# FNet and gMLP on one core: the first two DFT blocks loaded in halves, two tiles for each of the first rows of x

## The chip, the cores and the metric

The kernel runs on one core of one Trainium2 chip. The metric is the device time of one execution in microseconds (us). Five engines work side by side, each through its own instructions in the order written: the tensor engine (PE in the profile, its weight loads PEld), the vector engine (DVE), the scalar engine (ACT), GpSimd (POOL) and the sync engine (SP), which here only issues transfers. The transfers between memory and the core's own memory run beside them (DMA).

## The reference

Two layers with adaptive layer norms, of which the first concerns us: an FNet layer that takes the real part of a two-dimensional Fourier transform, written as products with DFT matrices. S is 2048, D is 512, all in float32.

```python
h = _layernorm(x, axis=-1) * (1 + ca) + sa
# _A_ref(h, ...):
a = jnp.einsum("bsd,ed->bse", x, dft_hid_re)
b = jnp.einsum("bsd,ed->bse", x, dft_hid_im)
y = jnp.einsum("ts,bse->bte", dft_seq_re, a) - jnp.einsum("ts,bse->bte", dft_seq_im, b)
...
x = x + ga * _A_ref(h, A_dft_seq_re, A_dft_seq_im, A_dft_hid_re, A_dft_hid_im)
h = _layernorm(x, axis=-1) * (1 + cb) + sb
x = x + gb * _B_ref(h, B_w_in, B_w_sp, B_b_sp, B_w_out)
```

`_B_ref` is a gMLP block (a projection with GELU, a gate through a 2048 x 2048 matrix, a projection back). It comes later in the kernel and the change does not touch it.

## The kernel before

The kernel multiplies along the sequence first: g = C x, for the real matrix `cr` and the imaginary one `ci`, where x is only normalized (scale and shift are folded into later matrices). A matrix is cut into blocks of 512 x 512; block b of the list `src` is the real part when b is even and the imaginary part when b is odd, as long as the first 512 output rows (t = 0) are made. Each block gives four **tiles**: tile n is a slice of 128 sequence positions, n = 4 b + k. Tile n is multiplied with row block s of x ("row s", 128 sequence positions by 512), and adds to four accumulators, one for each 128 columns of x. For t = 0 tiles 0 to 3 are the real tiles of rows 0 to 3, tiles 4 to 7 the imaginary tiles of the same rows, tiles 8 to 11 the real tiles of rows 4 to 7, and so on.

Float32 is reached in three passes of a faster format: both operands are split into a high and a low half, and high x high, high x low and low x high are added. So one tile takes 12 matmuls with 128 x 512, three for each accumulator. For tiles 0 to 3 (`n < 4` in `mm_a`, line 520 of the profile) they are ordered in three groups of four: first all four with `ah` and `hh`, then with `al` and `hh`, then with `ah` and `hl`. From tile 4 on `matmul3` (lines 96 to 98) gives three passes for one accumulator after the other.

What a tile needs:

- `prep_hi(n)`: the tile is transposed from the loaded block (`stage`) into `t` (DVE, L189), and ACT makes its high half `ah` (L268). With the fourth tile of a block the block's buffer is given up and the load of block b + 2 is issued (`load`). Two blocks fit, two `t`, four `ah`, three `al`.
- `prep_lo(n)`: DVE makes the low half `al` (L286).

What a row needs: statistics on DVE (`stats_first` L438 to L441 for rows 0 to 3, `stats_x` L104 to L106 for later ones), two or three small POOL instructions, its high half `hh` on ACT (`hi_first`, L459, with one column set by `one_first`, L465), the normalized row `xn` on ACT (`norm_x`, L120) and its low half `hl` on DVE (`lo_h`, L501).

The order of all this is written by hand (a manual schedule): up to the first tile a straight list of calls, which the diff shows, then a loop over tiles. In the loop, `prep(n)` calls `prep_hi(n + 3)` and `prep_lo(n + 2)`, `mm_a(n)` issues the matmuls, and `run(n)` issues whatever was put there by `at(n, f, ...)`. Loads of rows are issued by `load_x(g, ks)`, of blocks by `load`, or by `load_half`, which takes 64 of the 128 columns that the staged block has per partition and row group: pieces of 256 B where `load` has 512 B. The first two tiles of a block lie in its first half.

Of the kernel before, what the change touches and what calls it, by code (L numbers as in the profile page):

```python
# [8 lines left out]
F32 = mybir.dt.float32  # L9
# [4 lines left out]
P = 128  # L14
# [5 lines left out]
def fnet_gmlp_kernel(  # L20
# [32 lines left out]
    nc = tc.nc  # L53
# [5 lines left out]
    NS = S // P  # L59
# [14 lines left out]
    blocks = ctx.enter_context(pool("blocks"))  # L74
# [49 lines left out]
    def at(n, f, *a):  # L124
        fill.setdefault(n, []).append((f, a))
# [6 lines left out]
    def quad(a, r, k):  # L132
        return a[r * Q:(r + 1) * Q, k * Q:(k + 1) * Q]

    src = []
    for t in range(NQ):
        for g, j in ([(g, j) for g in range(NQ) for j in range(2)] if t == 0 else
                     [(g, j) for j in range(2) for g in range(NQ)]):
            src.append(quad((cr, ci)[j], t, g))
    N2 = 4 * len(src)  # L140
    N1 = N2 + 8
    YPROD = (6, 7, 4, 5, 3)
    N3 = N1 + 4 * len(YPROD)
    N4 = N3 + 4 * len(YPROD)
# [3 lines left out]
    NB0 = len(src) + 2  # L148
    stage, T, AH, AL = {}, {}, {}, {}
# [6 lines left out]
    def load_half(tile_, a, h, engs=(nc.sync,) * 4):  # L156

        v = a.rearrange("(b j) (a s) -> a j b s", j=32, a=4)
        for q in range(4):
            engs[q].dma_start(tile_[32 * q:32 * q + 32], v[q][:, :, 64 * h:64 * h + 64])  # L160
# [3 lines left out]
    def load(b):  # L164
        if b < len(src):
            stage[b] = blocks.tile([P, 16, P], F32, tag="stage", bufs=2, name=f"stage{b}")
            load_block(stage[b], src[b])
        elif b < len(src) + 2:
            j = b - len(src)
            XB.append(blocks.tile([P, 4, Q], F32, tag="stage", bufs=2, name=f"xb{j}"))  # L170
            for g in range(2):
                nc.sync.dma_start(XB[j][:, 2 * g:2 * g + 2], ht_d[g].rearrange("(k p) t -> p k t", p=P)[:, 2 * j:2 * j + 2])
                for kk in range(2):
                    TT[2 * j + kk, g] = XB[j][:, 2 * g + kk]
        elif 4 * (b - NB0) < NE - N4:
            i, gh = divmod(b - NB0, NQ)
            g, h = divmod(gh, 2)
            p = PROD[i]
            stage[b] = blocks.tile([P, 2, 16, 64], F32, tag="stage", bufs=2, name=f"stage{b}")
            for r in range(2):  # L180
                load_half(stage[b][:, r], s_d[S_OF[p], r, g] if p in S_OF else
                          quad(w_sp, r + (2 if p == 4 else 0), g + (2 if p == 1 else 0)), h)
# [68 lines left out]
    def prep_hi(n):  # L251
        if n >= NE or n in highs:
            return
        highs.add(n)
        if N2 <= n < N4:
            T[n] = form_t(n)
        else:
            b, k = divmod(n, 4) if n < N2 else (NB0 + (n - N4) // 4, (n - N4) % 4)
            if b != NB0:
                T[n] = blocks.tile([P, Q], F32, tag="t", bufs=2, name=f"t{n}")  # L260
            if b == NB0:
                assert n in T
            elif n >= N4:
                squares(T[n], stage[b][:, k % 2], k // 2)
            else:
                squares(T[n], stage[b], k)
        AH[n] = SE[2][:, n - N4] if N4 <= n < N4 + 4 else blocks.tile([P, Q], F32R, tag="ah", bufs=4, name=f"ah{n}")
        nc.scalar.activation(AH[n], T[n], AF.Copy)  # L268
        if not N2 <= n < N4 and k == 3:
            stage.pop(b)  # L270
            if b != NB0:
                load(b + 2)


    def prep_lo(n):
        if n >= NE or n in lows:
            return
        lows.add(n)
        if N2 <= n < N4 and n % 4 == 3:
            AL[n] = slot(0, f"al{n}", F32R) if slots else zrow[0].tile([P, Q], F32R, tag="z1u", bufs=6, name=f"al{n}")  # L280
        elif N4 <= n < N4 + 4:
            AL[n] = slot(9 + n - N4, f"al{n}", F32R)
        else:
            AL[n] = blocks.tile([P, Q], F32R, tag="al", bufs=3, name=f"al{n}")
        t = T.pop(n)
        nc.vector.tensor_tensor(AL[n], t, AH[n].bitcast(F32), op=ALU.subtract)  # L286
# [132 lines left out]
    X, XG, LN, NRM, h_hi, h_lo = {}, {}, {}, {}, {}, {}  # L419

    def load_x(g, ks=range(4), eng=nc.sync):

        if g not in XG:
            XG[g] = spool.tile([P, 4, D], F32, tag="x", bufs=2, name=f"x{g}")
        k0, k1 = ks[0], ks[-1] + 1
        v = x.rearrange("(g a k i) d -> g a i k d", g=NQ, a=4, i=32)
        for a in range(4):
            eng.dma_start(XG[g][32 * a:32 * a + 32, k0:k1, :], v[g, a][:, k0:k1, :])
        for k in ks:
            X[4 * g + k] = XG[g][:, k, :]  # L430
# [4 lines left out]
    def stats_first(s):  # L435

        m = spool.tile([P, 12], F32, tag="first", bufs=4, name=f"first{s}")
        nc.vector.bn_stats(m[:, :6], X[s])  # L438
        mv = m[:, 8:]
        nc.vector.bn_aggr(mv[:, :2], m[:, :6])  # L440
        nc.vector.tensor_scalar(mv[:, 1:2], mv[:, 1:2], EPS, None, op0=ALU.add)  # L441
        nc.gpsimd.tensor_tensor(mv[:, 2:3], mv[:, 1:2], mhalf, op=ALU.pow)
        nc.gpsimd.tensor_scalar(mv[:, 3:4], mv[:, 0:1], mv[:, 2:3], -1.0, op0=ALU.mult, op1=ALU.mult)
        NRM[s] = mv[:, 2:3], mv[:, 3:4]
# [11 lines left out]
    def hi_first(s):  # L456
        h_hi[s] = hpool.tile([P, ND, P], F32R, name=f"hh{s}")
        h = h_hi[s].rearrange("p k (a i) -> p k a i", i=32)
        nc.scalar.activation(h, X[s].rearrange("p (a k i) -> p k a i", a=4, i=32), AF.Identity,  # L459
                             bias=NRM[s][1], scale=NRM[s][0])  # L460
        if s:
            one_first(s)
# [19 lines left out]
    def norm_x(s):  # L482

        if s not in LN:
            LN[s] = spool.tile([P, D], F32, tag="xn", bufs=4, name=f"xn{s}")
        if s > 1:
            nc.gpsimd.memset(LN[s][:, 0:1], 1.0)
        apply(LN[s][:, 1:], X.pop(s)[:, 1:], NRM.pop(s))

# [8 lines left out]
    def lo_h(s):  # L498
        h_lo[s] = hpool.tile([P, ND, P], F32R, name=f"hl{s}")
        lo, h = parts_h(s, h_lo)  # L500
        nc.vector.tensor_tensor(lo, h, parts_h(s, h_hi)[0].bitcast(F32), op=ALU.subtract)  # L501
        LN.pop(s)


    GP, gt_hi, gt_lo, YP = {}, {}, {}, {}
# [2 lines left out]

    def mm_a(n):
        t, r = divmod(n, 8 * NQ)  # L510
        j, s = ((r // 4) % 2, r // 8 * 4 + r % 4) if t == 0 else (r // NS, r % NS)
        if s == 0:
            for k in range(ND):
                GP[t, j, k] = bank(4 * j + k if t == 0 else ring[0] % 6, f"gp{t}_{j}_{k}")
                ring[0] += t > 0
        ah, al = AH.pop(n), AL.pop(n)
        if n < 4:
            for a, b in ((h_hi[s], ah), (h_hi[s], al), (h_lo[s], ah)):
                for k in (1, 2, 3, 0):
                    nc.tensor.matmul(GP[0, 0, k], a[:, k, :], b, start=s == 0 and b is ah and a is h_hi[s], stop=False)  # L520
            return
        for k in range(ND):
            matmul3(GP[t, j, k], h_hi[s][:, k, :], h_lo[s][:, k, :], ah, al, s == 0, s == NS - 1)
        if s == NS - 1:
            for k in range(ND):
                ps = GP.pop((t, j, k))
                gt_hi[t, j, k] = GP_[0].tile([P, Q], F32R, tag=f"gh{j}_{k}", name=f"gh{t}_{j}_{k}")
                gt_lo[t, j, k] = GP_[0].tile([P, Q], F32R, tag=f"gl{j}_{k}", name=f"gl{t}_{j}_{k}")
                split(gt_hi[t, j, k], gt_lo[t, j, k], ps)
# [524 lines left out]
    load_half(stage[0][:, :, :64], src[0], 0, two)  # L1054
    load_two(1)
    nc.scalar.activation(sc, ones[:, :ND], AF.Silu)
    load_x(0, range(2, 4))
    load_half(stage[0][:, :, 64:], src[0], 1)
    load(1)
    load_x(1, range(2))  # L1060
    keep_busy(4, 5)
    for s in range(2):
        LN[s] = spool.tile([P, D], F32, tag="xn", bufs=4, name=f"xn{s}")
        nc.gpsimd.memset(LN[s][:, 0:1], 1.0)
    stats_first(0)
# [3 lines left out]
    stats_first(1)  # L1069
    prep_lo(0)  # L1070
    norm_x(0)
    prep_hi(1)
    lo_h(0)
    hi_first(1)
    stats_first(2)
    prep_lo(1)
    norm_x(1)
    prep_hi(2)
    lo_h(1)
    hi_first(2)  # L1080
    stats_first(3)
    prep_lo(2)
    norm_x(2)
    prep_hi(3)
    hi_first(3)
    norm_x(3)
    at(0, lo_h, 2)
    at(1, lo_h, 3)
    at(0, load_x, 1, range(2, 4))
    at(2, load_row)  # L1090
    at(9, silu_row)
# [31 lines left out]
    for j, turn, weigh, row, fold, hi in ((0, (25, 26, 27, 28), (29, 29, 30, 30), 26, (34, 34, 35, 36), (40, 37, 38, 39)),  # L1123
# [8 lines left out]
        n = weigh[3] + 1  # L1132
# [20 lines left out]
    for t in range(NQ):  # L1153
        n = 8 * NQ * (t + 1)
# [136 lines left out]
    for i, p in enumerate(PROD):  # L1291
        for k in range(8):
            n = NB[p] + 2 * k
# [11 lines left out]
    for f in range(NF):  # L1305
        n = N4 + 24 + 8 * f
# [109 lines left out]
```

## Time and profile before

| | |
|---|---|
| median of three runs | 933.13 us (932.32 to 933.69) |
| the profiled execution | 932.66 us |
| its span in the profile | 930.9 us |
| PE busy | 924.6 us, 99% |
| DVE busy | 737.3 us, 79% |
| first matmul of tile 0 / of tile 4 | 7.30 us / 20.59 us after the span's start |

Times in the profile count from the start of the span. A row of the timeline has the start, the duration, the engine, the line of the kernel, the operation with its output and inputs, and in brackets how long the engine was idle before it and what ended that. The difference of 1.76 us between span and time lies outside the profiled span.

### The profile page before, as it was taken

What the parts mean: (1) busy time and instruction counts of PE and PEld (TensorE: products, weight loads), DVE (VectorE), ACT (ScalarE), POOL (GpSimd) and SP (SyncE); (2) the same over time, 40 slices, a digit from 0 to 9 for tenths busy, and PEclk for the clock granted to TensorE, in tenths of its full rate; (3) what the DMA queues carried; (4) which work ended last, traced back from release to release, by engine and by line L of the source; (5) the groups of instructions that cost most, each with busy time, mean ns of one, the idle gap of its engine ahead of it and who ended that gap; (6) DMA issues with size and microseconds to landing.
All of it is one profiled execution on the core that took longest, in us unless ns stands there. A gap on an engine that the chain in (4) does not pass through costs nothing.

```text
span 930.9 us, 12343 instructions
## 1 busy us (share of the span) xinstructions
PE 924.6 (99%) x4053; PEld 760.7 (82%) x4053; DVE 737.3 (79%) x1217; ACT 409.6 (44%) x734; POOL 198.9 (21%) x376
## 2 busy tenths in 40 slices
PE   8999999999999999999999999999999999999998
PEld 5888888888888888888888888888888888888886
DVE  7789967788687677875668788899799789896762
ACT  5685424232132221322577877674544544331121
POOL 2420000224654165323512320331000000000000
PEclk9999999999999999999999999999999999999999
DMA  9995762856639977996464764444464555744651
GB/s 215 219 226 123 146 158 46 192 148 163 165 86 306 306 207 222 277 337 232 138 217 135 273 204 103 118 106 104 104 147 102 132 140 138 177 102 149 188 174 57
DMA packets 246976, 157.88 MB, mean 170 GB/s; under 512 B 140384, under 2 KB 214368, under 8 KB 246784
## 3 DMA queue, kind: packets, MB, share of 16 engines
q1 hardware_dynamic: 233248, 119.57, 52.0%
q0 software_dynamic: 12272, 36.86, 11.5%
q10 hardware_dynamic: 1392, 0.66, 0.2%
q8 instruction: 32, 0.52, 0.2%
q14 instruction: 32, 0.26, 0.1%
HBM read 120.33 MB, written 36.71 MB: 169 GB/s over the span
## 4 chain that ended last, share of the span: by engine, by line
PE 98%; DMA 1%; DVE 0%; SPq 0%; issue 0%; ACTq 0%; POOL 0%; ACT 0%; DVEq 0%
PE gp L96 12%; PE gp L97 12%; PE gp L98 12%; PE gw L97 10%; PE gw L98 10%; PE gw L96 10%; PE yp L98 3%; PE yp L96 3%; PE yp L97 3%; PE op L98 3%; PE op L97 3%; PE op L96 3%; PE fp L97 1%; PE fp L98 1%; PE fp L96 1%; PE z2s L98 1%
## 5 line engine op out<-in xcount | busy, mean ns | idle before, releaser
L268 ACT ACTIVATE ah<-t 128x512 fp32r<-128x512 f32 x236 | 149.1, 632 | 364.7 <-DVE t L189 252.5
L286 DVE TENSOR_TENSOR al<-t,ah 128x512 fp32r<-128x512 f32 x236 | 160.7, 681 | 52.6 <-PE gp L97 27.9
L97 PE MATMUL gp<-al,hh 128*128 128x512 f32 x496 | 193.0, 389 | 0.0
L96 PE MATMUL gp<-ah,hh 128*128 128x512 f32 x496 | 193.0, 389 | 0.0
L98 PE MATMUL gp<-ah,hl 128*128 128x512 f32 x496 | 192.9, 389 | 0.0
L189 DVE STREAM_TRANSPOSE t<-stage 128x512 f32<-128x512 f32 x236 | 165.7, 702 | 11.2 <-DMA stage<-in_A_dft_seq_re_dram 4.9
L97 PE MATMUL gw<-al,bh 128*128 128x512 f32 x400 | 155.6, 389 | 0.0
L98 PE MATMUL gw<-ah,bl 128*128 128x512 f32 x384 | 149.5, 389 | 0.0
L96 PE MATMUL gw<-ah,bh 128*128 128x512 f32 x384 | 149.4, 389 | 0.0
L98 PEld LDWEIGHTS gp<-ah,hl 128*128 128x128 f32 x496 | 93.1, 188 | 19.4
L96 PEld LDWEIGHTS gp<-ah,hh 128*128 128x128 f32 x496 | 93.1, 188 | 19.4
L97 PEld LDWEIGHTS gp<-al,hh 128*128 128x128 f32 x496 | 93.1, 188 | 19.4 <-DVE al L286 0.2
L97 PEld LDWEIGHTS gw<-al,bh 128*128 128x128 f32 x400 | 75.1, 188 | 15.5
L98 PEld LDWEIGHTS gw<-ah,bl 128*128 128x128 f32 x384 | 72.1, 188 | 15.5 <-DVE bl L919 0.5
L96 PEld LDWEIGHTS gw<-ah,bh 128*128 128x128 f32 x384 | 72.1, 188 | 15.0
L891 POOL DMA_DIRECT2D s_d<-sj x64 | 35.1, 548 | 106.8 <-DVE sj L883 82.4
L96 PE MATMUL yp<-hth,gh 128*128 128x512 f32 x128 | 49.8, 389 | 0.0
L97 PE MATMUL yp<-htl,gh 128*128 128x512 f32 x128 | 49.8, 389 | 0.0
L98 PE MATMUL yp<-hth,gl 128*128 128x512 f32 x128 | 49.8, 389 | 0.0
L636 POOL DMA_DIRECT2D ht_d<-hturn x62 | 41.0, 667 | 23.9 <-DVE hturn L632 18.5
L96 PE MATMUL op<-woh,uh 128*128 128x512 f32 x112 | 43.6, 389 | 0.0
L97 PE MATMUL op<-wol,uh 128*128 128x512 f32 x112 | 43.6, 389 | 0.0
(233 smaller groups left out, 1446.0 us busy)
## 6 DMA issues: line engine op xcount, KB each, us to landing
stage<-in_A_dft_seq_im_dram SPq DMA_DIRECT2D x64, 256.0 KB, 5.6
sj<-in_B_w_sp_dram SPq DMA_DIRECT2D x32, 512.0 KB, 6.8
s_d<-sj POOLq DMA_DIRECT2D x64, 256.0 KB, 4.2
stage<-s_d SPq DMA_DIRECT2D x128, 128.0 KB, 2.8
stage<-in_A_dft_seq_re_dram SPq DMA_DIRECT2D x60, 256.0 KB, 5.4
stage<-in_B_w_sp_dram SPq DMA_DIRECT2D x88, 128.0 KB, 2.9
wm<-in_w_mod_dram SPq DMA_DIRECT2D x16, 256.0 KB, 6.1
xr<-in_A_x_dram POOLq DMA_DIRECT2D x16, 256.0 KB, 4.5
```

Of the source, the lines that this page charges most:

```text
L96: nc.tensor.matmul(acc, ah, bh, start=first, stop=False, skip_group_check=go_on)
L97: nc.tensor.matmul(acc, ah, bl, start=False, stop=False, skip_group_check=go_on)
L98: nc.tensor.matmul(acc, al, bh, start=False, stop=last, skip_group_check=go_on)
L189: nc.vector.transpose(dst.rearrange("p (b i) -> p b i", i=32), block[:, :, 32 * k:32 * k + 32])
L268: nc.scalar.activation(AH[n], T[n], AF.Copy)
L286: nc.vector.tensor_tensor(AL[n], t, AH[n].bitcast(F32), op=ALU.subtract)
L636: eng.dma_start(v[a, i], ht[32 * a:32 * a + 32].rearrange("c (b r) -> c b r", r=32))
L891: nc.gpsimd.dma_start(s_d[m, r, g][b * P:(b + 1) * P, :], a)
```

## The change

The first two blocks are loaded half by half, in the order: first half of block 0, first half of block 1, rows 2 and 3 of x, second half of block 0, second half of block 1. The list `PAIRED` gives the first eight tiles a new meaning (block, slice): tiles 0 and 1 are the real and imaginary tile of row 0, tiles 2 and 3 those of row 1, tiles 4 and 5 the real tiles of rows 2 and 3, tiles 6 and 7 their imaginary ones. The grouped order of matmuls holds for tiles 0 to 5. The calls ahead of the loop, and those of the first three turns, are ordered anew; the first four `xn` are allocated, and their first columns set, ahead of everything. The fourth tile of block 0 is now tile 5, so the load of block 2 is issued there.

```diff
+    PAIRED = ((0, 0), (1, 0), (0, 1), (1, 1), (0, 2), (0, 3), (1, 2), (1, 3))
...
-            b, k = divmod(n, 4) if n < N2 else (NB0 + (n - N4) // 4, (n - N4) % 4)
+            b, k = PAIRED[n] if n < 8 else divmod(n, 4) if n < N2 else (NB0 + (n - N4) // 4, (n - N4) % 4)
...
-        if s > 1:
+        if s > 3:
             nc.gpsimd.memset(LN[s][:, 0:1], 1.0)
...
-        j, s = ((r // 4) % 2, r // 8 * 4 + r % 4) if t == 0 else (r // NS, r % NS)
+        j, s = PAIRED[n] if n < 8 else ((r // 4) % 2, r // 8 * 4 + r % 4) if t == 0 else (r // NS, r % NS)
...
-        if n < 4:
+        if n < 6:
             for a, b in ((h_hi[s], ah), (h_hi[s], al), (h_lo[s], ah)):
                 for k in (1, 2, 3, 0):
-                    nc.tensor.matmul(GP[0, 0, k], a[:, k, :], b, start=s == 0 and b is ah and a is h_hi[s], stop=False)
+                    nc.tensor.matmul(GP[0, j, k], a[:, k, :], b, start=s == 0 and b is ah and a is h_hi[s], stop=False)
             return
...
     load_half(stage[0][:, :, :64], src[0], 0, two)
     load_two(1)
     nc.scalar.activation(sc, ones[:, :ND], AF.Silu)
+    stage[1] = blocks.tile([P, 16, P], F32, tag="stage", bufs=2, name="stage1")
+    load_half(stage[1][:, :, :64], src[1], 0)
     load_x(0, range(2, 4))
     load_half(stage[0][:, :, 64:], src[0], 1)
-    load(1)
+    load_half(stage[1][:, :, 64:], src[1], 1)
     load_x(1, range(2))
     keep_busy(4, 5)
-    for s in range(2):
+    for s in range(4):
         LN[s] = spool.tile([P, D], F32, tag="xn", bufs=4, name=f"xn{s}")
         nc.gpsimd.memset(LN[s][:, 0:1], 1.0)
     stats_first(0)
...
     stats_first(1)
     prep_lo(0)
     norm_x(0)
+    lo_h(0)
     prep_hi(1)
-    lo_h(0)
     hi_first(1)
+    prep_lo(1)
+    prep_hi(2)
     stats_first(2)
-    prep_lo(1)
     norm_x(1)
-    prep_hi(2)
+    prep_lo(2)
     lo_h(1)
+    prep_hi(3)
     hi_first(2)
-    stats_first(3)
-    prep_lo(2)
-    norm_x(2)
-    prep_hi(3)
-    hi_first(3)
-    norm_x(3)
-    at(0, lo_h, 2)
-    at(1, lo_h, 3)
+    at(0, prep_lo, 3)
+    at(0, norm_x, 2)
+    at(0, prep_hi, 4)
+    at(0, stats_first, 3)
+    at(1, prep_lo, 4)
+    at(1, lo_h, 2)
+    at(1, hi_first, 3)
+    at(1, norm_x, 3)
+    at(2, lo_h, 3)
     at(0, load_x, 1, range(2, 4))
```

## The prediction

> **What bounds the kernel now.** I read the page's head first, then the waits of the tensor engine, then its timeline over the first 22 us, and then the timelines of the engines that feed it there.
>
> ```profile
> span 930.9 us, 12343 instructions
> PE 924.6 (99%) x4053; PEld 760.7 (82%) x4053; DVE 737.3 (79%) x1217; ACT 409.6 (44%) x734; POOL 198.9 (21%) x376
> ...
> PE gp L520 <- DVE hl L501: 0.7, 1, 0.7
> ...
> PEld gp L520 <- DVE hl L501: 2.1, 3, 1.1
> ...
> 7.30 1.19 PE L520 MATMUL gp<-ah,hh 128*128 128x512 f32 x4
> 8.74 1.20 PE L520 MATMUL gp<-al,hh 128*128 128x512 f32 x4 [0.26 <-DVE al L286]
> 9.94 1.20 PE L520 MATMUL gp<-ah,hl 128*128 128x512 f32 x4
> 10.98 1.12 PE L520 MATMUL gp<-ah,hh 128*128 128x512 f32 x4
> ...
> 17.84 1.08 PE L520 MATMUL gp<-ah,hh 128*128 128x512 f32 x4
> 18.76 1.08 PE L520 MATMUL gp<-al,hh 128*128 128x512 f32 x4
> ...
> 20.59 0.39 PE L96 MATMUL gp<-ah,hh 128*128 128x512 f32 x1
> ...
> 21.27 0.39 PE L96 MATMUL gp<-ah,hh 128*128 128x512 f32 x1
> ...
> 927.17 0.60 ACT last L1039
> ```
>
> The tensor engine is the bound. From 20.59 to 21.27 it starts three matmuls: 0.227 us each. From 20.59, where the fifth tile begins, to 927.17, where ACT takes up the last result, 906.6 us pass; of the 4053 matmuls 8 keep the engine busy at the start and 48 belong to the first four tiles, so 3997 remain, 0.2268 us each. Nothing stands behind 20.59 that could be won. Ahead of it, the first 48 matmuls need 48 x 0.227 = 10.9 us and take 20.59 - 7.30 = 13.3 us. So **2.4 us** is all that this change can win as long as the first matmul stays at 7.30: 0.26% of the profiled execution's 932.66 us. The stalls are waits for the vector engine (DVE): the weight loads waited three times, 2.1 us in all, for hl, the low half of a row of x.
>
> The change feeds each of rows 0 and 1 of x to two tiles, so that a row's preparation is needed half as often. Whether that helps is decided by DVE, whose instructions run in the order written:
>
> ```profile
> 8.01 0.68 DVE L286 TENSOR_TENSOR al<-t,ah 128x512 fp32r<-128x512 f32 x1
> 8.61 0.70 DVE L189 STREAM_TRANSPOSE t<-stage 128x512 f32<-128x512 f32 x1
> 9.23 0.65 DVE L501 TENSOR_TENSOR hl<-xn,hh 128x512 fp32r<-128x512 f32 x1
> 9.80 0.68 DVE L438 BATCH_NORM_STATS2 first<-x 128x6 f32<-128x512 f32 x1
> 10.81 0.68 DVE L286 TENSOR_TENSOR al<-t,ah 128x512 fp32r<-128x512 f32 x1
> 12.33 0.71 DVE L189 STREAM_TRANSPOSE t<-stage 128x512 f32<-128x512 f32 x1 [0.83 <-DMA stage<-in_A_dft_seq_re_dram]
> 16.93 0.71 DVE L189 STREAM_TRANSPOSE t<-stage 128x512 f32<-128x512 f32 x1 [0.18 <-DMA stage<-in_A_dft_seq_im_dram]
> 21.50 0.71 DVE L189 STREAM_TRANSPOSE t<-stage 128x512 f32<-128x512 f32 x1
> ...
> 22.70 0.69 DVE L104 BATCH_NORM_STATS2 bstx<-x 128x6 f32<-128x512 f32 x1
> 24.40 0.71 DVE L189 STREAM_TRANSPOSE t<-stage 128x512 f32<-128x512 f32 x1
> 29.73 1.28 DVE L501 TENSOR_TENSOR hl<-xn,hh 128x512 fp32r<-128x512 f32 x2
> ```
>
> I call the transposition of tile n Tn, its low half al n, and the low half of row s hl s. The rows are al0, T1, hl0, statistics of row 2, al1, T2, T4, T7, statistics of row 4, T8, and hl4 with hl5. Pitches, start to start: al 0.60, T 0.62, hl 0.57, the three statistics instructions 1.01.
>
> The row that decides is the last. hl4 is ready at 29.73 + 0.65 = 30.4. The ninth tile (n = 8, the first on row 4) starts at 20.59 + 48 x 0.2267 = 31.47 and wants hl4 with its third matmul, at 31.93. So DVE is only **1.5 us** ahead of the tensor engine there, and no order of the first eight tiles takes work from DVE ahead of hl4: the same transpositions, low halves and statistics stand before it, in another order. Whatever idle time DVE gains past 1.5 us lands on the tensor engine.
>
> **The change part by part.** ACT, POOL, the loads and the DMA:
>
> ```profile
> 6.62 0.63 ACT L268 ACTIVATE ah<-t 128x512 fp32r<-128x512 f32 x1
> 7.15 0.19 ACT L465 ACTIVATE hh<-ones 128x1 fp32r<-128x1 f32 x1
> 7.24 0.80 ACT L120 ACTIVATE xn<-x,first 128x511 f32<-128x511 f32 x1
> ...
> 10.05 0.81 ACT L459 ACTIVATE hh<-x,first 128x512 fp32r<-128x512 f32 x1
> ...
> 17.36 0.80 ACT L120 ACTIVATE xn<-x,first 128x511 f32<-128x511 f32 x1
> 18.07 0.61 ACT L268 ACTIVATE ah<-t 128x512 fp32r<-128x512 f32 x1
> ...
> 10.98 0.92 POOL L442 TENSOR_TENSOR first<-first,mhalf 128x1 f32<-128x1 f32 x1 [0.96 <-DVE first L441]
> 12.00 0.26 POOL L443 TENSOR_SCALAR first<-first 128x1 f32<-128x1 f32 x1
> ...
> 4.78 1.78 SPq L428 DMA_DIRECT2D x<-in_A_x_dram  x4
> 6.60 2.02 SPq L160 DMA_DIRECT2D stage<-in_A_dft_seq_re_dram  x4
> 8.66 2.74 SPq L154 DMA_DIRECT2D stage<-in_A_dft_seq_im_dram  x4
> ...
> 15.87 1.91 SPq L154 DMA_DIRECT2D stage<-in_A_dft_seq_re_dram  x4
> ...
> x<-in_A_x_dram SPq DMA_DIRECT2D x1, 128.0 KB, 3.0
> ...
> 8.13 4.07 DMA stage<-in_A_dft_seq_re_dram
> ...
> 9.00:12.00 3.00, 3.00 (x13) 2.00 (x13) 2.42 (x6) 2.35 (x4) 1.84 (x4) 1.00 1.01 225
> 12.00:17.00 5.00, 4.22 (x18) 2.88 (x17) 4.21 (x9) 3.37 (x6) 1.51 (x5) 1.00 1.18 228
> ```
>
> *Loads.* The queue of loads is as before up to 4.78. There it carried rows 2 and 3 of x (512 KB), the second half of the first block (512 KB, last landed at 8.13 + 4.07 = 12.2) and the second block (1 MB, whose first use, T4, starts at 16.93). Now the first half of the second block takes the first place; rows 2 and 3, the second half of the first block, and the second half of the second block follow. The bytes up to 16.9 are the same. Four issues of a half take 2.02 us, so the last one starts about 6.3; with the 3.0 us to landing of the issue that had this place (rows 2 and 3) it is there at 9.3, with the 4.07 us of the next one at 10.4. I take 9.6, since the place in the queue is that of the rows. The second half of the first block then lands at about 14.6, half way from 12.2 to 16.9, and nothing waits for it.
>
> *Tile 1.* It now wants T1 from the second block and no row but row 0. hl0 moves ahead of T1 and runs at 8.61, so the third group of tile 0 comes at about 9.7 and not 9.94. T1 at 9.6 ends at 10.3 (DVE idle 0.4), ah1 follows on ACT to 10.98, and al1 starts at 11.03 (DVE idle 0.8). The tensor engine starts tile 1 at **11.03**, where it stood at 10.98: here nothing is won, since the wait for row 1 becomes one for the half block.
>
> *Tiles 1 to 7 on the tensor engine.* After tile 1 the rows are no longer what it waits for. With the 0.92 us that a group of four took (17.84 to 18.76), and 0.1 more behind a stall, tile 2 starts at 13.9, tile 3 at 16.7, tile 4 at 19.4, tile 5 at 22.2.
>
> *DVE and ACT meanwhile*, each instruction at the pitch of its row, 0.05 us from one engine to another: T2 11.6, statistics of row 2 12.3, al2 13.3, hl1 13.9, T3 14.4 to 15.15; ah3 ends at 15.83, so al3 starts at 15.88 (DVE idle 0.8); T4 16.5, statistics of row 3 17.1, al4 18.1, hl2 18.7, T5 19.3 to 20.0. hl3 comes next, and its inputs form a chain: the statistics end at 18.2, POOL takes 0.92 + 0.1 + 0.26 (to 19.57), ACT 0.81 + 0.25 for hh3 and its first column, then 0.80 for xn3, to 21.4. So hl3 starts at 21.43 (DVE idle **1.5**, the largest). Then T6 22.0, al5 22.6 to 23.3, T7 23.35 (its buffer is al5's source), al6 24.0, statistics of rows 4 and 5 24.6, and T8 could start at 24.6 + (24.40 - 22.70) = 26.3. al5 is wanted at 23.1 and comes at 23.35, so tile 6 starts at 25.2. Before, it started at 20.59 + 24 x 0.2267 = 26.03: the tensor engine is **0.85 us ahead**.
>
> *The third block's load* is issued behind the last tile of the first block. That was tile 3 (15.87); now it is tile 5, at 20.05, behind the load of rows 6 and 7, which it used to precede. By bytes: 3 MB at 16.9, rows 4 to 7 (1 MB) at 228 GB/s to 21.5, the block to 26.1; late issue can add some tenths. I take T8 at **26.4**. From T8 to hl4 DVE runs without a gap in the rows of before, 29.73 - 24.40 = 5.33: hl4 starts at 31.73, ends at 32.4, and the tensor engine has it at 32.43, where it had started that matmul at 31.93. Tile 8 would have started at 30.6, so a new stall of 1.35 us takes back the 0.85 and 0.5 more. hl5, 0.6 us later, is in time for tile 9.
>
> *The rest* costs nothing by these rows: the two more clearings on POOL stand ahead of everything; the tiles 4 and 5 in groups are the same 24 matmuls; behind tile 8 DVE and DMA carry what they did. Behind hl4 the pressure ends: before hl6, wanted two tiles (5.4 us) later, stand hl5, two transpositions and two low halves, 3.0 us by the pitches.
>
> **Sum:** -0.85 + 1.35 = **+0.5 us** on the profiled execution: 933.2. The median of the three runs, 933.13, lies 0.47 above the profiled 932.66, so the forecast for a median is **933.6**. A measurement of this kernel (932.32 to 933.69) tells about 0.2%, 1.87 us, from no change.
>
> **A page on the DMA.** The windows show 225 GB/s from 9 to 12 us, while halves (pieces of 256 B, 64 columns of four bytes) are in flight, and 228 GB/s from 12 to 17, when whole blocks (512 B) are. The Trainium skill ("DMA: Bandwidth & Descriptors", section Specifications) gives 512 B as the least transfer for full rate, below which the engine reads, modifies and writes. By that rule the second block in halves would come slower, which speaks against the change; this trace does not bear it out as a large loss.
>
> **The rivals.**
>
> *Halves flow slower, and the third block is late (slower).* Against the window's rate stands one pair of rows: the rows of x had landed at 6.1 + 3.0 = 9.1 (6.1 is the start of the last of their four issues), the half behind them at 12.2, so 512 KB took 3.07 us, where the whole block took 4.7 for 1 MB (12.2 to 16.9). Two halves at 3.07 are 1.4 us more than a block. It decides if T8 waits for the third block past 26.3; each 0.1 us then goes through DVE to hl4 and to the end. T8 at 27.8, the end 1.9 us later: **935.0**. At half the block's rate (9.4 us in place of 4.7) the loads would be late by 4.7 us and the end by 5.2, some 938. The rule on the Trainium skill's page (DMA: Bandwidth & Descriptors, Specifications) speaks for the whole of this price. For it: DVE has no slack left. Against it: the 225 GB/s.
>
> *DVE keeps up (faster).* If T1's half lands at 9.3, the chain through POOL is shorter and the third block is there in time, DVE's idle times (0.4, 0.8, 0.8, 1.5) shrink by the 1.7 us that the stall at tile 8 needs. Then only tile 1's start counts: five tiles in groups of 2.76 and two of 2.72 from 11.03 put tile 8 at 30.3, 1.2 us earlier: **931.9**. For it: the two waits of 0.8 hang on one ACT instruction each. Against: the 1.5 is a chain of five instructions that the new order itself puts late.
>
> *Nothing moves.* The head's stall only changes its place, and hl4 comes at the old 31.9: 933.1. It is inside my forecast's range.
>
> **How the numbers follow.** Within 0.9 us of the forecast's +0.5 (the errors of some tenths each at T1, T8 and hl3): 0.62. DVE keeps up, -0.4 to -1.5: 0.18; a gain past 1.87 would need more than three quarters of the 2.4 and gets 0.05 within that. Slower by the halves or the late block: 0.20, of which 0.15 past +1.87. Faster 0.05, same 0.80, slower 0.15. The range goes from 931.8 (the second rival and a tenth) to 935.2 (the first price of the slow halves and two tenths); some 0.07 lies below it and 0.13 above.
>
> **What would show it.** Right: tile 1's first group near 11.0, tile 6 near 25.2; a wait of the weight loads or of the tensor engine for hl L501 of over a microsecond near 31 to 32; a DVE idle time before hl3 that ends with ACT's xn; T8 near 26.4. Wrong on the fast side: tile 8 without a wait, hl4 before 31. Wrong on the slow side: T1 after 10.4, or T8 idle for DMA stage past 27. The forecast as a whole is wrong if the tenth tile (n = 9), at 34.2 before, starts outside 33.3 to 35.6.

## The result and the profile after

The changed kernel takes 934.71 us (median of 10 runs, 934.31 to 936.04), the kernel before 932.60 us in the same comparison (931.93 to 933.69): a ratio of **1.0026** (95% interval 1.0017 to 1.0035), 2.1 us slower. A second comparison gave 934.22 against 932.33, 1.0019 (1.0010 to 1.0028). The forecast was 933.6 with a range of 931.8 to 935.2: the result lies in the range, on its slow side, and four times as far from the time before as forecast (+2.1 against +0.5 us).

The page of the changed kernel begins so, with the span's length and the busy times:

```profile
span 933.7 us, 12349 instructions
PE 925.4 (99%) x4053; PEld 761.1 (82%) x4053; DVE 737.8 (79%) x1217; ACT 409.6 (44%) x734; POOL 198.7 (21%) x376
```

The tensor engine's work is the same (4053 matmuls); its busy time is 0.8 us longer, the span 2.8 us. The profiled execution took 935.5 us, 0.8 above the median, so it shows somewhat more than the typical loss. The engine's own waits for tiles in the changed kernel (total, times, longest; one more belongs to the matmuls that keep it busy at the start):

```profile
PE gp L98 <- DVE hl L502: 1.4, 1, 1.4
PE gp L97 <- DVE al L287: 1.2, 1, 1.2
PE gp L521 <- DVE al L287: 0.2, 1, 0.2
```

Before, the waits were in the first four tiles. Now two of the three are under L97 and L98, in tiles that `matmul3` makes, which had no wait at all before. (All lines moved down by one: L501 of before is L502.) The timeline of the tensor engine, changed kernel:

```profile
7.62 1.49 PE L521 MATMUL gp<-ah,hh 128*128 128x512 f32 x4
...
11.03 1.20 PE L521 MATMUL gp<-ah,hh 128*128 128x512 f32 x4
...
23.35 1.20 PE L521 MATMUL gp<-al,hh 128*128 128x512 f32 x4 [0.18 <-DVE al L287]
...
25.30 0.39 PE L96 MATMUL gp<-ah,hh 128*128 128x512 f32 x1
...
29.64 0.50 PE L97 MATMUL gp<-al,hh 128*128 128x512 f32 x1 [1.24 <-DVE al L287]
...
34.34 0.50 PE L98 MATMUL gp<-ah,hl 128*128 128x512 f32 x1 [1.38 <-DVE hl L502]
...
36.75 0.39 PE L96 MATMUL gp<-ah,hh 128*128 128x512 f32 x1
...
929.89 0.60 ACT L1040 ACTIVATE last<-op 128x512 f32<-128x512 f32 x1 [8.21 <-PE op L98]
```

Tile 1 starts at 11.03 and tile 6 at 25.30: up to here the new order works, and tile 6 is 0.7 us ahead of its time before (26.03). Then tile 7 waits 1.24 us for al7 and tile 8 waits 1.38 us for hl4. The third matmul of tile 8 starts at 34.34; before, it started at 31.92. From there to the last ACT instruction (the last row) it is 895.55 us now and was 895.25, so 2.4 of the 2.7 us by which that instruction is later arise ahead of 34.34. The row at 36.75 is the start of tile 9. DVE shows why both came late:

```profile
9.60 0.71 DVE L190 STREAM_TRANSPOSE t<-stage 128x512 f32<-128x512 f32 x1 [0.42 <-DMA stage<-in_A_dft_seq_im_dram]
11.01 0.69 DVE L287 TENSOR_TENSOR al<-t,ah 128x512 fp32r<-128x512 f32 x1 [0.70 <-ACT ah L269]
...
15.83 0.69 DVE L287 TENSOR_TENSOR al<-t,ah 128x512 fp32r<-128x512 f32 x1 [0.70 <-ACT ah L269]
...
21.41 0.69 DVE L502 TENSOR_TENSOR hl<-xn,hh 128x512 fp32r<-128x512 f32 x1 [1.44 <-ACT xn L120]
...
28.30 0.71 DVE L190 STREAM_TRANSPOSE t<-stage 128x512 f32<-128x512 f32 x1 [2.07 <-DMA stage<-in_A_dft_seq_re_dram]
28.93 0.65 DVE L287 TENSOR_TENSOR al<-t,ah 128x512 fp32r<-128x512 f32 x1
...
33.61 1.28 DVE L502 TENSOR_TENSOR hl<-xn,hh 128x512 fp32r<-128x512 f32 x2
```

The rows are T1, al1, al3, hl3, T8, al7 and hl4 with hl5. The first four stand where the prediction put them (9.6, 11.03, 15.88, 21.43). T8 does not: DVE is ready for it at 26.23 and waits 2.07 us for block 2. al7 and all up to hl4 stand behind T8 on the same engine.

The issues of loads in the changed kernel's timeline, a piece of its chain of work (start, duration), and its windows, whose last number is the GB/s that the DMA moved:

```profile
13.10 3.77 SPq L429 DMA_DIRECT2D x<-in_A_x_dram  x8
19.99 1.91 SPq L155 DMA_DIRECT2D stage<-in_A_dft_seq_re_dram  x4
```
```profile
21.41 6.36 DMA stage<-in_A_dft_seq_re_dram
```
```profile
9.00:12.00 3.00, 2.92 (x13) 2.10 (x12) 1.89 (x4) 1.54 (x3) 0.27 (x1) 1.00 0.98 233
12.00:17.00 5.00, 5.00 (x23) 4.11 (x23) 4.23 (x9) 3.14 (x6) 1.19 (x2) 1.00 1.04 246
...
19.00:20.00 1.00, 1.00 (x6) 0.84 (x5) 0.97 (x2) 0.45 (x1) 0.42 (x2) 1.00 0.20 43
20.00:21.00 1.00, 1.00 (x6) 0.81 (x5) 0.00 (x0) 0.97 (x3) 0.00 (x0) 1.00 0.00 1
```

The windows in which the halves came, with some rows of x among them, moved 233 and 246 GB/s, and rows 4 to 7 were issued by 16.9. Then nothing more could be issued until T5 freed the buffer at 19.96, and from 20 to 21 us the DMA moved 1 GB/s. The last part of block 2, issued at 21.41, took 6.36 us to land, at 27.77; T8 started 0.53 us later, and the profile shows nothing else that it waited for.

### The profile page after: what moved, and what is told of

It reads as the page before. It is cut to its first block, busy times and chain, and to the rows that moved or that the text cites. A ratio compares the mean times of both kernels' runs of the same rounds, so it can differ in the third digit from the quotient of the medians.

```text
span 933.7 us, 12349 instructions
## 1 busy us (share of the span) xinstructions
PE 925.4 (99%) x4053; PEld 761.1 (82%) x4053; DVE 737.8 (79%) x1217; ACT 409.6 (44%) x734; POOL 198.7 (21%) x376
## 4 chain that ended last, share of the span: by engine, by line
PE 96%; DMA 1%; SPq 1%; DVE 1%; issue 0%; ACTq 0%; ACT 0%; DVEq 0%
PE gp L98 12%; PE gp L97 12%; PE gp L96 12%; PE gw L98 10%; PE gw L96 10%; PE gw L97 10%; PE yp L96 3%; PE yp L98 3%; PE yp L97 3%; PE op L98 3%; PE op L97 3%; PE op L96 3%; PE fp L97 1%; PE fp L96 1%; PE fp L98 1%; PE z2s L97 1%
## 5 line engine op out<-in xcount | busy, mean ns | idle before, releaser
L98 PE MATMUL gp<-ah,hl 128*128 128x512 f32 x488 | 190.0, 389 | 1.4 <-DVE hl L502 1.4
L97 PE MATMUL gp<-al,hh 128*128 128x512 f32 x488 | 190.0, 389 | 1.2 <-DVE al L287 1.2
L96 PE MATMUL gp<-ah,hh 128*128 128x512 f32 x488 | 190.0, 389 | 0.0
L97 PE MATMUL gw<-al,bh 128*128 128x512 f32 x400 | 155.6, 389 | 0.0
L98 PE MATMUL gw<-ah,bl 128*128 128x512 f32 x384 | 149.6, 390 | 0.0
L98 PEld LDWEIGHTS gp<-ah,hl 128*128 128x128 f32 x488 | 91.6, 188 | 20.8 <-DVE hl L502 1.8
L97 PEld LDWEIGHTS gp<-al,hh 128*128 128x128 f32 x488 | 91.6, 188 | 20.6 <-DVE al L287 1.8
L97 PEld LDWEIGHTS gw<-al,bh 128*128 128x128 f32 x400 | 75.1, 188 | 15.7
L98 PEld LDWEIGHTS gw<-ah,bl 128*128 128x128 f32 x384 | 72.1, 188 | 15.6 <-DVE bl L920 0.5
L97 PE MATMUL yp<-htl,gh 128*128 128x512 f32 x128 | 49.8, 389 | 0.0
L98 PE MATMUL yp<-hth,gl 128*128 128x512 f32 x128 | 49.8, 389 | 0.0
L97 PE MATMUL op<-wol,uh 128*128 128x512 f32 x112 | 43.6, 389 | 0.0
```

The lines of the kernel that those rows point to most:

```text
L96: nc.tensor.matmul(acc, ah, bh, start=first, stop=False, skip_group_check=go_on)
L97: nc.tensor.matmul(acc, ah, bl, start=False, stop=False, skip_group_check=go_on)
L98: nc.tensor.matmul(acc, al, bh, start=False, stop=last, skip_group_check=go_on)
```

## The experiments

Two theories. **Late block**: the load of block 2 hangs on T5, which moved from 15.87 to 19.99; the transfers run dry, T8 waits, and al7 and hl4 stand behind it on DVE. **Order**: the waits that the new order has on DVE itself (0.7 + 0.7 + 1.4 us) cost the time. Each median stands with that of the kernel before on the same chip; each ratio has its 95% interval (it is taken from all runs and can differ by up to 0.0002 from the quotient of the two medians). "Third matmul" is that of tile 8, in the profiled execution; single profiles shift as a whole by some tenths, since the first matmul came between 7.3 and 8.1 us.

| run | us, before us | ratio (interval) | T8 | third matmul |
|---|---|---|---|---|
| before | | | 24.40 | 31.92 |
| changed, first | 934.71, 932.60 | 1.0026 (1.0017-1.0035) | 28.30 | 34.34 |
| changed, again | 934.22, 932.33 | 1.0019 (1.0010-1.0028) | 27.43 | 33.47 |
| early_block | 933.84, 933.06 | 1.0008 (0.9999-1.0017) | 27.04 | 33.09 |
| before_late | 933.59, 933.06 | 1.0007 (0.9998-1.0016) | 26.37 | 32.42 |
| al7_first | 933.85, 933.06 | 1.0010 (1.0001-1.0019) | 27.07 | 32.67 |
| rows_first | 935.23, 933.06 | 1.0029 (1.0019-1.0040) | 27.02 | see text |
| row_later | 934.44, 932.33 | 1.0023 (1.0014-1.0032) | 26.68 | 32.74 |
| hl3_later | 933.93, 932.09 | 1.0019 (1.0010-1.0028) | 26.79 | 32.84 |
| order_only | 933.72, 932.09 | 1.0019 (1.0010-1.0027) | 27.32 | 32.92 |
| t5_early | 933.57, 932.33 | 1.0013 (1.0004-1.0022) | 26.70 | 32.76 |
| best | 932.32, 932.33 | 0.9998 (0.9990-1.0007) | 25.56 | 31.16 |
| best2 | 931.53, 932.09 | 0.9993 (0.9984-1.0002) | 24.42 | 30.69 |

**early_block.** Block 2 goes into a buffer that is free.

```diff
+    stage[2] = spool.tile([P, 16, P], F32, tag="wb", bufs=1, name="stage2")
+    load_block(stage[2], src[2])
     keep_busy(4, 5)
...
-            if b != NB0:
+            if b not in (NB0, 0):
                 load(b + 2)
```

> The changed kernel, with block 2 loaded into a buffer that is free (the one that a later column load uses), issued right behind rows 4 and 5 of x; all else in the changed order. Theory 'late block' (the load of block 2 is issued behind T5, at 19.99 in place of 15.87, the transfers run dry, T8 waits 2.07 us, and al7 and hl4 stand behind T8 on DVE): T8 starts near 26.25 without a wait for a transfer, hl4 ends near 32.2, tile 8's third matmul is near 32.3 (34.34 in the changed kernel, 31.93 before), and the time is 2.0 us under the changed kernel's, about 1.0003 of the time before. Theory 'order' (the new order's own idle times on DVE, 0.7 + 0.7 + 1.4 us before al1, al3 and hl3, cost the time and the load does not matter): no change from the changed kernel, about 1.0023 of the time before.

1.0008 against 1.0026 and 1.0019 of the changed kernel, which speaks for the late block, though the recovered part is 1.0 or 1.7 us, by which of the two comparisons one takes, and not 2.0, and the intervals touch in the first and overlap in the second. In the profile the block's issues begin at 16.09; T8 starts at 27.04 in a head that began 0.4 us late, still behind a wait of 0.40 us that the profile gives to another load (`crow`, the row load), for which no run shows the reason. The wait for al7 is gone. hl4 comes too late even so:

```profile
8.06 1.19 PE L521 MATMUL gp<-ah,hh 128*128 128x512 f32 x4 [0.99 <-ACT ah L269]
...
33.09 0.50 PE L98 MATMUL gp<-ah,hl 128*128 128x512 f32 x1 [1.32 <-DVE hl L502]
```

So with block 2's load issued in time a wait of 1.3 us is left at tile 8, about the one that the prediction had priced (1.35), though 0.40 of it can come from T8's own wait.

**before_late.** The converse: in the kernel before, only block 2's load is made late (behind hl3, and so behind rows 6 and 7).

```diff
-            if b != NB0:
+            if b not in (NB0, 0):
                 load(b + 2)
...
+    mark_d = dram.tile([1, 32], F32, name="mark_d")
+    at(1, lambda: nc.sync.dma_start(mark_d, h_lo[3][:1, 0, :32].bitcast(F32)))
+    at(1, load, 2)
     at(2, load_row)
```

> The kernel before, with nothing changed but that block 2's load is issued late: behind a small store of 128 bytes that waits for hl3 (18.95 us). Theory 'late block': issued near 19.5, T8 near 27.5 in place of 24.40, hl4 near 33.5, tile 8's third matmul 1.3 to 1.9 us later than 31.93, time 1.0014 to 1.0020 of the time before. Theory 'order': DVE has no new idle time but this wait, and the tensor engine runs on as before: 1.0000.

T8 moved from 24.40 to 26.37, and a wait at tile 8 appeared that was not there before:

```profile
26.37 0.71 DVE L189 STREAM_TRANSPOSE t<-stage 128x512 f32<-128x512 f32 x1 [1.94 <-DMA stage<-in_A_dft_seq_re_dram]
...
32.42 0.50 PE L98 MATMUL gp<-ah,hl 128*128 128x512 f32 x1 [0.31 <-DVE hl L501]
```

The 1.5 us by which DVE was ahead took up most of it. The block landed about a microsecond sooner than expected, so the price is 0.5 us in the profile, and 1.0007 in the times, which is not clear of no change. The wait shows the mechanism; the times do not, and they miss the 1.0014 to 1.0020 expected. The price is small as long as DVE has its lead.

**rows_first.**

```diff
+    at(4, prep_lo, 7)
+    for f in (stats_x, norm_x, hi_h):
+        at(4, f, 4)
+        at(4, f, 5)
+    at(5, lo_h, 4)
+    at(5, lo_h, 5)
-    for s, n in ((4, 4), (5, 4), (6, 6), (7, 6), (8, 10), (9, 10)):
+    for s, n in ((6, 6), (7, 6), (8, 10), (9, 10)):
```

> The changed kernel, with block 2's load as late as in it, but al7 and the whole preparation of rows 4 and 5 (statistics, xn, hh) ordered ahead of T8 and hl4, hl5 directly behind it. Theory 'late block': T8 still waits, to 28.3, but nothing that tile 7 needs and only a short subtraction that tile 8 needs stands behind it; no wait of the tensor engine of over 0.3 us after tile 5; tile 8 starts near 30.8 (31.47 before), time 0.7 us under the time before, 0.9993 of it. Theory 'order': DVE's idle times before hl3 and the rest are still there, so a wait near tile 8 remains and the time is 1.001 of the time before or more.

Its median is above the changed kernel's in either comparison (the intervals overlap). The chain through POOL and ACT now stood ahead of T8's own followers:

```profile
30.19 1.29 DVE L502 TENSOR_TENSOR hl<-xn,hh 128x512 fp32r<-128x512 f32 x2 [2.45 <-ACT hh L497]
...
32.73 0.50 PE L97 MATMUL gp<-al,hh 128*128 128x512 f32 x1 [0.99 <-DVE al L287]
38.86 0.50 PE L96 MATMUL gp<-ah,hh 128*128 128x512 f32 x1 [0.54 <-ACT hh L497]
```

DVE stood 2.45 us for hh4 and hh5, and T9 and al8 waited behind that. The third matmul of tile 8 came at 33.07, and the last row shows one more wait behind it. The first expectation was wrong: it counted what was moved forward and not what that pushed back. The second holds in its number, but by this new wait, so the run does not tell the theories apart.

**al7_first.**

```diff
+    at(4, prep_lo, 7)
     for s, n in ((4, 4), (5, 4), (6, 6), (7, 6), (8, 10), (9, 10)):
```

> The changed kernel with al7 alone ordered ahead of the statistics of row 4, and so ahead of T8. If the two waits of the tensor engine (1.24 us for al7 in tile 7, 1.38 us for hl4 in tile 8) are one lateness met twice, so that hl4 alone sets the end: the first wait goes, the second grows to about 2.6 us, time as the changed kernel, 1.0023 of the time before. If they add up as two costs: the first goes and the second stays, 1.2 us less, 1.0010.

The wait for al7 is gone, but the one before hl4 did not grow: 0.6 us, after 0.4 for hh4. In this profile block 2 also landed sooner (T8 at 27.07 with the load issued at 19.95). The time, 1.0010, is that of the second expectation, but the waits are those of neither: al7's 0.6 us now fill time in which DVE had waited for the block (before T8 no wait is left in this profile), which neither counted. The interval overlaps that of the changed kernel (1.0019).

**after_again, row_later.** The same kernel once more, and with the 256 KB row load issued behind block 3.

```diff
-    at(2, load_row)
+    at(4, load_row)
```

> The changed kernel once more, beside the following ones. Block 2's last transfer landed 6.36 us after its issue in one profile and 5.2 us in that of the kernel with al7 first, with the same issue time, so T8 is expected between 27.0 and 28.3 and the time at 1.002 to 1.003 of the time before.

> The changed kernel, with the 256 KB row load (crow) that is issued right behind block 2 moved behind block 3. Theory 'shared': transfers issued close together share the rate, so the row's 256 KB lie inside block 2's landing; without them T8 starts up to 1.2 us earlier (256 KB at 215 GB/s), near 27.0 against a run of the changed kernel at 28.2, time 0.0007 to 0.0013 lower than the changed kernel's. Theory 'in turn': transfers land in order of issue, the row comes behind the block anyway, and nothing changes.

The changed kernel's T8 came at 27.43 this time, as expected. Without the row load behind it, the last two parts of block 2 landed 4.9 us after issue (median) and not 5.6, and T8 started 0.75 us sooner:

```profile
27.43 0.71 DVE L190 STREAM_TRANSPOSE t<-stage 128x512 f32<-128x512 f32 x1 [1.68 <-DMA stage<-in_A_dft_seq_re_dram]
```
```profile
26.68 0.71 DVE L190 STREAM_TRANSPOSE t<-stage 128x512 f32<-128x512 f32 x1 [0.92 <-DMA stage<-in_A_dft_seq_re_dram]
```

The first line is the changed kernel again, the second row_later. That is as transfers sharing the rate would do. The Trainium skill says that transfers run on the same 16 engines and interleave ("DMA: Bandwidth & Descriptors", section Issuing engines are not separate DMA queues). These runs do not show it: in order_only, with the row load in its old place, the last two parts took 5.1 us, and T8 came between 26.79 and 28.30 in the profiles with that load, a spread wider than the 0.75 us. The times show no gain (1.0023 against 1.0019), and the profile of row_later was its fastest execution. The share of the row load stays open.

**t5_early.** T5 ahead of the statistics of row 3, so that block 2's load is issued at 17.65.

```diff
+    at(0, prep_hi, 5)
     at(0, stats_first, 3)
```

> The changed kernel, with T5 and ah5 ordered before the statistics of row 3, so that block 2's load is issued 2.2 us earlier (near 17.75), before the transfers run dry. Theory 'late block': T8 does not wait for the block any more and starts near 26.2, time 1.0003 to 1.0008 of the time before, as with the block loaded early into a free buffer. Theory 'order': the idle time of 1.4 us before hl3 stays, or grows by the 0.6 us that T5 takes before the statistics, and the time stays at 1.002 or above.

Both theories were half right. T8 no longer waits for a transfer, although the DMA stood nearly empty here too (57 GB/s from 17 to 19 us): what counts is when the load is issued. But T5 pushes row 3 back, and DVE waits longer before hl3:

```profile
21.89 0.69 DVE L502 TENSOR_TENSOR hl<-xn,hh 128x512 fp32r<-128x512 f32 x1 [2.06 <-ACT xn L120]
...
26.70 0.71 DVE L190 STREAM_TRANSPOSE t<-stage 128x512 f32<-128x512 f32 x1
```

The wait grew from 1.44 to 2.06 us, T8 stands at 26.70, and 1.0013 is left.

**hl3_later, order_only.** The load left late and the order changed, so that DVE does not stand before hl3: first hl3 alone behind T6 and al5, then also T7 ahead of hl3 and al7 ahead of the statistics of row 4.

```diff
# hl3_later
-    at(2, lo_h, 3)
+    at(3, lo_h, 3)
# order_only
-    at(2, lo_h, 3)
+    at(3, prep_hi, 7)
+    at(3, lo_h, 3)
...
+    at(4, prep_lo, 7)
```

> The changed kernel with hl3 behind T6 and al5, and nothing else. T5 and block 2's load stay where they are. Theory 'late block': what DVE wins ahead of T8 is lost again in the longer wait for block 2, T8 stays where it was (27.4 to 28.3) and so does the time, 1.0019 to 1.0026. Theory 'order': T8 comes earlier by what is won, up to 0.7 us, and the time falls to 1.0012 to 1.0019.

> The reordered version that equalled the kernel before, without its early T5: T7 ahead of hl3, hl3 behind T6 and al5, al7 ahead of the statistics of row 4, block 2's load as late as in the changed kernel. If the load decides: T8 waits to 27.0 or later, though DVE is ready near 25.5, and as al7 is no longer behind it hl4 ends near 32.5, time 1.0008 to 1.0014, as with al7 first. If the order decides: as the reordered version with the early load, 0.9998.

Both stayed at 1.0019, the changed kernel's value; for order_only that is above what either theory expected. The two rows are order_only's al5 and T8:

```profile
22.09 0.69 DVE L287 TENSOR_TENSOR al<-t,ah 128x512 fp32r<-128x512 f32 x1 [1.30 <-ACT ah L269]
...
27.32 1.31 DVE L190 STREAM_TRANSPOSE t<-stage 128x512 f32<-128x512 f32 x2 [0.40 <-DMA stage<-in_A_dft_seq_re_dram]
```

The idle time of DVE had only moved. ah5, the high half of tile 5, stands behind xn3 on ACT, so DVE now stood 1.30 us before al5 (in hl3_later too) where it had stood 1.44 us before hl3. It was ready for T8 hardly sooner: 10.1 us after the start of al3 in hl3_later and 10.4 in both profiles of the changed kernel; order_only took 10.9, with al7 ahead of T8. So these runs do not show what an order without that idle time is worth with the load left late.

**best.** order_only with the early T5 of t5_early.

> The changed kernel with T5 early as in t5_early, hl3 behind T6, al5 and T7 so that DVE does not stand idle for xn3, and al7 ahead of the statistics of row 4. By the late block and by the order alike: block 2 issued near 17.8 and landed by 25.2, DVE idle before hl3 0.3 us or less, T8 near 25.7, hl4 ready near 31.0, tile 8's third matmul near 31.0 (31.93 before), so 0.9 us faster than before, 0.9990 to 0.9996. If a third cause holds the tensor engine, the third matmul of tile 8 stays at 32 or later.

```profile
20.53 0.65 DVE L287 TENSOR_TENSOR al<-t,ah 128x512 fp32r<-128x512 f32 x1
...
25.56 1.30 DVE L190 STREAM_TRANSPOSE t<-stage 128x512 f32<-128x512 f32 x2
...
31.16 0.50 PE L98 MATMUL gp<-ah,hl 128*128 128x512 f32 x1 [0.27 <-DVE hl L502]
```

T8 (with T9) at 25.56 and the third matmul at 31.16, 1.76 us earlier than in order_only in both; the time went from 1.0019 to 0.9998, two microseconds for one line, `at(0, prep_hi, 5)`. The line does two things. Block 2's load is issued at 17.81 in place of 20.22, and ah5 now comes ahead of xn3 on ACT, so that DVE no longer stands before al5 (first row). By the rows neither would have been enough alone: in order_only the block let T8 start at 27.32 at the earliest, however soon DVE was ready, and DVE was ready at 26.92 (T8's start less its wait), so that an earlier block alone would have moved T8 by 0.40 us. That is worked out from one profile; no run has the one without the other. The third matmul is 0.8 us ahead of before, but the time equals that of before within its interval, and its median is a little above the 0.9990 to 0.9996 expected.

**best2.** In addition T2 ahead of T1, and T3 ahead of the statistics of row 2.

```diff
+    prep_hi(2)
     prep_hi(1)
     hi_first(1)
     prep_lo(1)
-    prep_hi(2)
-    stats_first(2)
     norm_x(1)
     prep_lo(2)
-    lo_h(1)
     prep_hi(3)
+    stats_first(2)
+    lo_h(1)
     hi_first(2)
```

> The reordered version with early load, and T2 ahead of T1 and T3 ahead of the statistics of row 2, so that DVE does not wait before T1, al1 and al3 (0.5 + 0.7 + 0.7 us). T5 near 16.0, block 2 issued near 16.6, landed before 24.5, T8 near 24.5, hl4 before 30.3, and no wait of the tensor engine after tile 1: tile 8's third matmul near 30.8 (31.93 before, 31.16 in the version without this), time 0.9985 to 0.9995. If something other than DVE's idle time and the block holds it, no better than 0.9998.

```profile
9.05 1.30 DVE L190 STREAM_TRANSPOSE t<-stage 128x512 f32<-128x512 f32 x2
11.05 1.29 DVE L287 TENSOR_TENSOR al<-t,ah 128x512 fp32r<-128x512 f32 x2 [0.70 <-ACT ah L269]
...
24.42 1.30 DVE L190 STREAM_TRANSPOSE t<-stage 128x512 f32<-128x512 f32 x2
...
30.69 0.39 PE L98 MATMUL gp<-ah,hl 128*128 128x512 f32 x1
```

The tensor engine has no wait after the start of tile 1, and the third matmul is at 30.69, 1.23 us ahead of before; time and matmul are as expected. The median is 0.56 us under that of before (931.53 against 932.09), 0.9993, and the interval (0.9984 to 1.0002) just reaches no change: the version is likely a little faster than both kernels, and these runs cannot tell it from before.

## Why the prediction was right or wrong

- **Bound: right.** After 40 us the tensor engine never waits for another engine, in any of these profiles. The ceiling of 2.4 us was not put to the test: no version came more than 1.23 us ahead at tile 8. From the third matmul of tile 8 to the last ACT instruction it takes 895.2 to 895.7 us in every one of which the table gives that matmul.
- **Tile 1 gains nothing: right.** 11.03, as forecast; the wait for row 1 became one for the half block. That T1 fits to 0.01 us is luck: the forecast chose 9.6 between 9.3 and 10.4, and in the other profiles of the new order T1 started between 9.12 and 10.01 (best2, where T2 goes first, left aside).
- **The replay of DVE, ACT and the tensor engine to tile 6: right** within 0.1 us (T1, al1, al3, hl3, T5 and tile 6 at 9.60, 11.01, 15.83, 21.41, 19.26 and 25.30).
- **The third block's load: mis-sized, and this is the step that failed.** The issue time was right (19.99 against 20.05). The landing was counted by bytes, as if the DMA had never stopped: 26.1, with some tenths for a late issue. But the DMA had run dry before the load could be issued (43 and 1 GB/s in the two windows before 21), and T8 started at 28.30 and 27.43 and not at 26.4. Rows of before spoke against the count in two ways. First, the landing after the issue: its four parts of block 2 took 5.8 us (median) and the last one 6.6, in a DMA that kept moving (203 to 242 GB/s from 17 to 24 us); added to the issue of the last part, 21.41, that is 28.0, and 27.77 was measured. Second, the bytes: the prediction has 3 MB (3.15 million bytes) there at 16.9, but the windows of before, 201, 225 and 228 GB/s for 9, 3 and 5 us, add up to 3.6 million by 17, so part of rows 4 and 5 had come too. Counted so, the 4 MB (4.19 million bytes) ahead of block 2 are there near 19.5 and not 21.5, an estimate from these windows, and the DMA stands empty at 20.05. The rows of before, the four parts, the last part, and the first window:

```profile
stage<-in_A_dft_seq_re_dram SPq DMA_DIRECT2D x4, 256.0 KB, 5.8
...
stage<-in_A_dft_seq_re_dram SPq DMA_DIRECT2D x1, 256.0 KB, 6.6
...
0.00:9.00 9.00, 7.21 (x13) 3.27 (x14) 4.16 (x10) 3.64 (x6) 2.15 (x11) 1.00 0.79 201
```

- **From T8 to hl4: right.** 5.31 us against 5.33. With T8 at 28.30 the forecast's own sum gives +0.5 + 1.9 = +2.4, and the profile shows 34.34 - 31.92 = 2.42 us; the medians are +2.1 and +1.9.
- **al7 behind T8: not named.** It brought the first of the two waits (1.24 us). It did not add to the sum: its place on DVE is inside the 5.33 us from T8 to hl4, and hl4 came later still. In al7_first, where it stood ahead of T8, hl4 set the end all the same, 4.87 us behind T8.
- **The rivals.** The slow rival's price (a late block, T8 near 27.8, the end 1.9 us later) is about what happened, but not its cause. Halves did not flow slower: the first row below, from 6.6 to 8.5 us of the changed kernel, has nearly only packets under 512 B, at 241 GB/s, the second, from 11.4 to 14 us of before, nearly only packets from 512 B to 2 KB, at 223. The Trainium skill gives 512 B as the least transfer for full rate ("DMA: Bandwidth & Descriptors", section Specifications), by which the 256 B pieces would come slower; the trace disagrees in this case. So it is luck that the result lies in the range: its slow end was put there for a cause that did not occur. "DVE keeps up" did not happen, for the reason given against it: the 1.5 us before hl3 were 1.44. best2, where DVE does keep up, comes to the lead that this rival had at tile 8 (1.2 us), with a median 0.56 us under that of before.

```profile
DMA packets 1634, 0.46 MB, mean 241 GB/s; under 512 B 1604, under 2 KB 1604, under 8 KB 1634
...
DMA packets 1157, 0.57 MB, mean 223 GB/s; under 512 B 43, under 2 KB 1157, under 8 KB 1157
```

- **The signs.** The starts of tiles 1 and 6 and the wait before hl3 came as named. But DVE stood idle for T8's block past 27 (to 28.30 and 27.43), which the prediction had named as wrong on the slow side, and the tenth tile started at 36.75 and 35.87 in the two profiles, outside the 33.3 to 35.6 by which the forecast as a whole was to be judged. By its own signs the account of the third block was wrong, though the time fell into the range.
- **The chances.** The first comparison is slower by 0.26% and the second by 0.19%, on either side of the bound of 0.2%. The 0.80 for "same" was too sure, since the sum had no slack at the one step that failed, and the rows of before that bear on it were not used.

## What to carry to other kernels

When a reordering moves the last use of a buffer, ask which load is issued by it, and whether the DMA still has work until then; count the landing from the issue, not by bytes, where it has not. On engines that run in the written order, find the instruction with the least lead behind the change and add up all idle time that the new order puts before it: a lead of 1.5 us decided here, some 20 us behind the edit. When an instruction is moved out of a wait, look where the wait goes: two such moves brought nothing, since it went from hl3 to al5. An earlier load in the changed order brought 0.6 to 1.7 us (t5_early, early_block), and the version with both gained two and more.

## What the runs showed of the hardware

A block of 1 MB issued at the same time (19.5 to 20.2 us) by the same four instructions let T8 start between 26.79 and 28.30 in six profiles, and in both of these T8 waited for it: a load into a DMA that had run dry had a spread of over a microsecond. Its last part landed 6.36 us after its issue in one profile, about as late as the last part of the same block in before (6.6), where the DMA had not run dry. Pieces of 256 B came as fast as pieces of 512 B (241 GB/s against 223 of before). And the first matmul, ahead of which little differs between these kernels, came between 7.30 and 8.06 us from profile to profile.
